# Batch 1's packed queries in the first p load, batch 4's keys and queries turned by the DMA crossbar, and a new order of the work

## The chip, the cores and the metric

The kernel runs on one core of one Trainium2 chip. The metric is the device time of that core in microseconds (us), as the median of the runs shown. The core's engines are TensorE (PE), VectorE (DVE), ScalarE (ACT), GpSimd (POOL) and SyncE (SP); each works through its own queue of instructions in order, and 16 DMA engines move the data. Here POOL issues nearly all loads and SP nearly all stores and the transposing DMAs.

## The reference

```python
def sm_attn(qq, kk, vv):
    s = scale * np.matmul(qq, kk.transpose(0, 1, 3, 2))      # scale = 1/8
    a = np.exp(s - np.max(s, axis=-1, keepdims=True))
    a = a / (np.sum(a, axis=-1, keepdims=True) + 1e-09)
    return np.matmul(a, vv)

p_packed = sm_attn(p, k, v)              # p [8, 8, 32, 64]; q, k, v [8, 8, 576, 64]
o = sm_attn(q, p_packed, p_packed)       # [8, 8, 576, 64]
x = o.transpose(0, 2, 1, 3).reshape(4608, 512)
h = x @ w_in                             # [512, 2048]
out = (np.maximum(h, 0.0) ** 2) @ w_out  # [2048, 512], out is [4608, 512]
```

Inputs and output are float32. There are 8 batches of 8 heads. For each head, 32 learned "packed queries" p attend to 576 keys, and the 576 queries then attend to the 32 packed results. Two dense layers with a squared ReLU between them follow, over all 4608 tokens.

## The kernel before

**Stages of a batch.** The work is cut into pieces with short names, and the prediction uses these names. For a batch b and a half qd of its heads:

- Loads by POOL: Lk (keys), Lv (values), Lq (queries), LWI and LWO (w_in and w_out); functions `dma_kq` (655), `dma_v` (674), `x_v` (679), `dma_w_in` (691), `dma_w_out` (695). LP is a load of p (`p_load`, 635), P its cast (642), PT its turn on VectorE (646).
- Tk and Tq turn keys and queries so that the head dimension lies on the partitions. For batches 0 to 4 VectorE does it (`tr_k`, L705, and `tr_q`, L702). For the batches in XBAR (5, 6, 7) a transposing DMA does it, which SP issues (`xbar`, L711); p then goes the same way, in two such DMAs, PX.0 and PX.1 (`xbar_p`, L715), and the values come in six loads and two zero fills rather than two loads.
- S1 is p times keys (L733; L749 in a crossbar batch), MX the row maximum (L752), EX the exponential (L760), E the turn of the result (L766), EC its copy, PV the product with the values (L780), RC and XN the normalisation (L784, L787), XM the turn of p_packed (L796; in a crossbar batch also L799), XC its copy.
- M multiplies p_packed with w_in ahead of time (L810): the second attention's output and the first layer become one product. Four pieces, each copied out by MC (L611 on ACT, L613 on DVE).
- S2 is queries times p_packed (L827; L837 in a crossbar batch); SI, SM, SU, SE, SS, SN and SO are its softmax and its turn (L848 to L875).
- F (batches 0 and 1, L912) or F1 (L884) is the first layer; R and Q or SQ the ReLU and the square (L894, L896, L902, L904, L920 to L932). F2 (L938) is the second layer for a tile of 128 tokens, 16 matmuls; FC copies its result out (L611, L613), and ST stores it (`store`, L950, two DMAs a tile). For tokens of batches 2 to 7 the second layer goes by groups of 256 tokens with sums of operands (GS, L990; WS, L983; products GP, L1005, 8 matmuls a piece; GC, L1025 and L611, adds them up).

**What sets the order.** Nothing is a loop over batches at run time: a list scheduler (`Plan`, lines 31 to 217) orders all pieces while the program is built. Every piece has one or more engines with a cost in us, the pieces that it follows, the PSUM halves that it takes, and a due level; TABLE (from line 228) holds an offset to the level of each piece. TURN is a cost that the planner adds where TensorE goes from one form of matmul to another. `run` (199) then emits the pieces in planned order, engine by engine, and puts filler matmuls (L617) into planned idle time of TensorE before the second layer begins.

The planned order is only an order on each engine. At run time an instruction waits for the data that it reads, for the buffer that it writes, and for the slot of its DMA queue; nothing waits for a planned time.

**Loads.** ORDER gives their sequence; x and y are the halves of batch 0's queries, a the parts of w_in, b those of w_out:

```python
ORDER = ("k0 v0 x0 a0 y0 a1 a2 a3 k1 b0 b1 v1 b2 q1 b3 b4 b5 b6 b7 "
         "k2 v2 q2 k3 v3 q3 k4 v4 q4 k5 v5 q5 k6 v6 q6 k7 v7 q7")
```

An entry "p4" in ORDER would give the load behind it, in the plan, the batch's Tk, Tq and, for the first crossbar batch, PX as pieces to follow.

**The packed queries.** p comes in three loads: batch 0 (64 KB, issued by ACT at the very start), batch 1 (64 KB, issued by SP behind a gate, a one-column write of VectorE) and batches 2 to 7 (issued by SP behind a second gate). They land in space that the gT sums and the w_out sums use later (gS, wS).

Of the kernel before, what the change touches and what calls it, by code (L numbers as in the profile page):

```python
# [11 lines left out]
F32 = mybir.dt.float32  # L12
BF16 = mybir.dt.bfloat16

P = 128
D = 64
# [10 lines left out]
TURN = 0.098  # L27
# [14 lines left out]
class Plan:  # L42
# [170 lines left out]
    def fills(self, a, b):  # L213
        if b - a < 0.7:
# [6 lines left out]
         "k2 v2 q2 k3 v3 q3 k4 v4 q4 k5 v5 q5 k6 v6 q6 k7 v7 q7")  # L221

KHW = 2
GROUPS = (2, 3, 4, 5, 6, 7)
XBAR = (5, 6, 7)
XTURN = (5, 6, 7)

TABLE = {'o': {'Lk.0.0i': 118.526678, 'Lk.0.1i': -2.097617, 'Lk.0.0': 127.028834, 'LP.0': -27.492568, 'Lk.0.1':
# [295 lines left out]
def kernel_impl(tc, q, k, v, p, w_in, w_out, out):  # L524
# [23 lines left out]
    with ExitStack() as ctx:  # L548
# [517 lines left out]
        for x in ORDER.split():  # L1066
# [29 lines left out]
            elif x[0] == "a":  # L1096
                for i in range(2):
                    for qd in QDS:
                        load(f"LWI.{n}.{i}.{qd}", 0.7, lambda n=n, i=i, qd=qd: dma_w_in(n, i, qd), 0.6)
# [297 lines left out]
```

## Time and profile before

| quantity | value |
|---|---|
| runs | 238.29, 238.25, 237.69 us; median 238.25 |
| profiled execution | 239.7 us |
| its span, first to last instruction | 237.9 us |
| mean granted TensorE clock in it | 0.997 |
| share of the chain that ended last, TensorE | 77% |
| data moved by DMA | 34.06 MB |

The table's span is what the profile's own times count from; the 1.8 us between it and the execution's time lie before the first and behind the last instruction. Where a view lists groups, it gives the line of the kernel, the engine, the operation, the output and inputs, the count, and then the busy time and the mean duration in ns. Where it lists stretches, it gives for each engine the busy time and, in brackets, the number of instructions.

### The profile page before, as it was taken

What the parts mean: (1) busy time and instruction counts of PE and PEld (TensorE: products, weight loads), DVE (VectorE), ACT (ScalarE), POOL (GpSimd) and SP (SyncE); (2) the same over time, 40 slices, a digit from 0 to 9 for tenths busy, and PEclk for the clock granted to TensorE, in tenths of its full rate; (3) what the DMA queues carried; (4) which work ended last, traced back from release to release, by engine and by line L of the source; (5) the groups of instructions that cost most, each with busy time, mean ns of one, the idle gap of its engine ahead of it and who ended that gap; (6) DMA issues with size and microseconds to landing.
All of it is one profiled execution on the core that took longest, in us unless ns stands there. A gap on an engine that the chain in (4) does not pass through costs nothing.

```text
span 237.9 us, 6410 instructions
## 1 busy us (share of the span) xinstructions
PE 223.7 (94%) x2635; PEld 159.6 (67%) x2635; DVE 201.4 (85%) x337; ACT 149.6 (63%) x242; POOL 59.9 (25%) x107
## 2 busy tenths in 40 slices
PE   7778798999999999999999999999999999999991
PEld 5555564435644547677678878788676888888781
DVE  3678797899799999999978999999999997868240
ACT  3314795179858999959797363449979987400100
POOL 9778546333343658600000000000000000000000
PEclk9999999999999999999999999999999999999998
DMA  7999999999999999998147697860314000615316
GB/s 226 175 179 176 190 204 204 204 195 248 239 204 229 213 224 212 199 203 129 38 96 140 141 163 165 189 130 4 88 44 92 3 0 0 146 33 110 69 42 178
DMA packets 46732, 34.06 MB, mean 143 GB/s; under 512 B 25392, under 2 KB 38448, under 8 KB 46704
## 3 DMA queue, kind: packets, MB, share of 16 engines
q0 software_dynamic: 19456, 18.03, 47.5%
q1 hardware_dynamic: 26576, 15.05, 29.7%
q10 hardware_dynamic: 672, 0.59, 1.0%
q8 instruction: 20, 0.33, 0.6%
q14 instruction: 8, 0.07, 0.1%
HBM read 37.22 MB, written 9.44 MB: 196 GB/s over the span
## 4 chain that ended last, share of the span: by engine, by line
PE 77%; DMA 10%; ACT 4%; POOL 2%; DVE 2%; issue 1%; SPq 1%; DVEq 0%; POOLq 0%
PE pb L1005 29%; PE ps L884 20%; PE pb L938 12%; DMA w_in_b<-in_moe_w_in_dram 6%; PE ps L810 3%; PE ps L912 3%; PE ps L938 3%; DMA v_b<-in_v_dram 3%; DMA out_dram<-o_sb 2%; ACT r_b L920 2%; PE pb L956 1%; PE ps L827 1%; PE ps L780 1%; PE ps L733 1%; POOL w_in_b L693 1%
## 5 line engine op out<-in xcount | busy, mean ns | idle before, releaser
L894 ACT ACTIVATE r_b<-ps 128x576 bf16<-128x576 f32 x86 | 50.1, 663 | 12.5 <-PE ps L884 12.2
L884 PE MATMUL ps<-a,M 128*128 128x288 bf16 x384 | 53.0, 286 | 0.0
L884 PEld LDWEIGHTS <-M 128*128 128x128 bf16 x384 | 37.3, 98 | 11.5 <-DVE a L875 0.3
L1005 PEld LDWEIGHTS <-gT 128*128 128x128 bf16 x384 | 37.1, 98 | 7.3 <-issue 2.5
L938 PE MATMUL pb<-w_out_b,gT 128*128 128x512 bf16 x144 | 39.1, 380 | 0.0
L611 ACT CAST M<-ps 128x1024 bf16<-128x1024 f32 (+1 forms) x29 | 26.5, 950 | 10.2 <-PE ps L810 8.8
L950 POOL DMA_DIRECT2D out_dram<-o_sb x2 | 1.1, 570 | 122.7 <-DVE o_sb L1025 121.5
L1005 PEld LDWEIGHTS <-gS 128*128 128x128 bf16 x288 | 27.6, 98 | 4.6 <-issue 0.9
L611 ACT COPY o_sb<-pb 128x512 f32<-128x512 f32 (+1 forms) x21 | 12.0, 571 | 29.4 <-PE pb L1005 18.8
L904 DVE TENSOR_TENSOR gT<-r_b 128x1152 bf16<-128x1152 bf16 x36 | 26.4, 747 | 3.6 <-ACT r_b L894 3.5
L1025 DVE TENSOR_TENSOR o_sb<-o_sb,pb 128x512 f32<-128x512 f32 x30 | 20.3, 677 | 9.3 <-PE pb L1005 8.5
L938 PEld LDWEIGHTS <-gT 128*128 128x128 bf16 x176 | 16.0, 98 | 15.9 <-issue 3.0
L1005 PE MATMUL pb<-wS,gT 128*128 128x256 bf16 x192 | 23.9, 273 | 0.5 <-DVE o_sb L1025 0.5
L1005 PE MATMUL pb<-wS,gS 128*128 128x256 bf16 x192 | 24.0, 273 | 0.0
L1005 PE MATMUL pb<-w_out_b,gT 128*128 128x256 bf16 x192 | 23.3, 273 | 0.0
L912 PE MATMUL ps<-a,M 128*128 128x256 bf16 (+3 forms) x160 | 19.5, 262 | 2.1 <-DVE M L613 0.6
L912 PEld LDWEIGHTS <-M 128*128 128x128 bf16 x160 | 13.9, 97 | 8.1 <-issue 2.5
L920 ACT ACTIVATE r_b<-ps 128x512 bf16<-128x512 f32 (+2 forms) x25 | 15.5, 662 | 3.8 <-PE ps L912 3.0
L861 ACT ACTIVATE e<-s 128x1152 bf16<-128x1152 f32 (+4 forms) x11 | 10.0, 909 | 10.3 <-DVE s L858 10.2
L760 ACT ACTIVATE e<-ps,n 128x576 bf16<-128x576 f32 x16 | 11.8, 744 | 7.4 <-DVE n L752 5.9
L617 PE MATMUL pb<-o_sb 128*128 128x256 bf16 x91 | 13.2, 299 | 1.1 <-DVE o_sb L620 1.1
L902 ACT ACTIVATE gT<-r_b 128x1152 bf16<-128x1152 bf16 x12 | 14.0, 1177 | 0.1
(88 smaller groups left out, 337.0 us busy)
## 6 DMA issues: line engine op xcount, KB each, us to landing
out_dram<-o_sb SPq DMA_DIRECT2D x65, 128.0 KB, 3.1
kq_b<-in_k_dram POOLq DMA_DIRECT2D x14, 288.0 KB, 9.8
kq_b<-in_q_dram POOLq DMA_DIRECT2D x10, 288.0 KB, 6.5
w_in_b<-in_moe_w_in_dram POOLq DMA_DIRECT2D x16, 128.0 KB, 6.1
w_out_b<-in_moe_w_out_dram POOLq DMA_DIRECT2D x8, 256.0 KB, 9.2
v_b<-in_v_dram POOLq DMA_DIRECT2D x5, 320.0 KB, 10.3
v_b<-in_v_dram POOLq DMA_DIRECT2D x12, 128.0 KB, 8.2
v_b<-in_v_dram POOLq DMA_DIRECT2D x5, 256.0 KB, 10.3
```

The source lines that it names most:

```text
L611: nc.scalar.copy(dst, src)
L617: nc.tensor.matmul(half(7)[:, :2 * P], lhsT=zero[:, :P], rhs=zero, start=True, stop=True)
L760: nc.scalar.activation(e_out(qd) if b in XBAR else e1[:, qd, :S], ps1[b, qd], ACT.Exp, bias=n1[b % 2][:, qd:qd + 1], accum_out=d1[b % 2][: ...
L884: nc.tensor.matmul(t[:, c], lhsT=M[b % 2][:, qd, fb * FB:(fb + 1) * FB], rhs=a2[b % 2][:, qd, c * HALF:(c + 1) * HALF], start=(qd == 0), s ...
L894: nc.scalar.activation(dst, src, ACT.Relu)
L902: nc.scalar.activation(dst, r, ACT.Square)
L904: eng.tensor_tensor(out=dst, in0=r, in1=r, op=ALU.mult)
L912: nc.tensor.matmul(t[:, c, m * w:(m + 1) * w], lhsT=M[b % 2][:, qd, fb * FB:(fb + 1) * FB], rhs=a2[b % 2][:, qd, o:o + w], start=(qd == 0) ...
L920: nc.scalar.activation(dst, ph["h", b, x, j], ACT.Relu)
L938: nc.tensor.matmul(po[t], lhsT=gT[:, fb, n0:n0 + P], rhs=w_out_b[:, fb, :], start=(fb == 0), stop=(fb == NFB - 1))
L1005: nc.tensor.matmul(pz[g, k][:, i], lhsT=a[:, f, i * P:(i + 1) * P], rhs=w[:, f], start=(k not in ON and h == 0 and f == 0 and i == 0), sto ...
L1025: nc.vector.tensor_tensor(out=oC(g, i, j), in0=oC(g, *src), in1=pz[g, z], op=ALU.add)
```

## The change

Four things change in the code.

1. p is loaded in two parts instead of three: batches 0 and 1 at the start by ACT (128 KB), batches 2 to 7 by SP. The load of batch 1 by SP and its gate go.
2. XBAR is (4, 5, 6, 7) instead of (5, 6, 7). Batch 4's keys and queries are turned by SP's transposing DMAs instead of VectorE; its values come in six loads and two zero fills; its S1, XM and S2 take the crossbar form; PX.0 and PX.1 hold one batch more.
3. "p4" stands behind q4 in ORDER.
4. Costs in the planner and TURN are new, and every offset in TABLE is new. The order on all engines differs with it.

```diff
-TURN = 0.098
+TURN = 0.111
...
-         "k2 v2 q2 k3 v3 q3 k4 v4 q4 k5 v5 q5 k6 v6 q6 k7 v7 q7")
+         "k2 v2 q2 k3 v3 q3 k4 v4 q4 p4 k5 v5 q5 k6 v6 q6 k7 v7 q7")
...
-XBAR = (5, 6, 7)
+XBAR = (4, 5, 6, 7)
...
-            p_f += [gS[:, i].rearrange("p a n -> p (a n)")[:, :2 * NQD * D].bitcast(F32) for i in range(2)]
+            p_f.append(gS[:, 0].rearrange("p a n -> p (a n)")[:, :2 * 2 * NQD * D].bitcast(F32))
...
-        for i, n, gate in ((1, 1, "MX.0.1"), (2, 6, "XQ.1")):
+        for i, n, gate in ((1, 6, "XQ.1"),):
...
-        for i, (b0, b1) in enumerate(((0, 1), (1, 2), (2, B))):
+        for i, (b0, b1) in enumerate(((0, 2), (2, B))):
...
-                add(f"S1.{b}", [("PE", 0.3, lambda u0, u1, b=b: x1_mm(b, [u0, u1]))], [f"Tk.{b}.0", f"Tk.{b}.1", "PX.0", "PX.1"],
+                add(f"S1.{b}", [("PE", 0.26, lambda u0, u1, b=b: x1_mm(b, [u0, u1]))], [f"Tk.{b}.0", f"Tk.{b}.1", "PX.0", "PX.1"],
...
-        p_load(0, 0, 1, nc.scalar)
+        p_load(0, 0, 2, nc.scalar)
```

The other costs that change are those of LP.0 (0.25 to 0.5), three of the w_in loads (0.45 more each), S1 (0.56 to 0.51), PV (0.5 to 0.3), XM (0.17 to 0.33 and 0.07 to 0.06), M (0.235 to 0.216) and S2.

In instructions as built: TensorE has 32 matmuls fewer at L733 and at L827, 32 more at L749, 16 more at L837, two more at L799, and 13 more fillers (104 instead of 91). VectorE has two turns fewer at L705 and two fewer at L702. POOL has six more loads of values in place of two, and two more zero fills. SP has four more transposing DMAs of keys and queries.

In the built order, SP's queue around batch 4 reads: the load of p for batches 2 to 7; the stores of tiles 0, 1, 2, 3, 4, 5, 7; Tk.4.0, PX.0, PX.1, Tk.4.1, Tq.4.0, Tq.4.1; the stores of tiles 8, 6, 11, 12, 9, 10; Tk.5.0, Tk.5.1. Before, PX.0 and PX.1 stood behind Tk.5.0 and Tk.5.1. On TensorE, S1.4 now stands behind the first seven F2 matmuls of tile 6 and then F1.2, one F2 matmul more among them, and one GP piece; before, it stood ahead of F1.2 (at 78.57 us).

More of the change, by code (lines that the diff above doesn't have):

```diff
@@ L220 @@
 ORDER = ("k0 v0 x0 a0 y0 a1 a2 a3 k1 b0 b1 v1 b2 q1 b3 b4 b5 b6 b7 "
-         "k2 v2 q2 k3 v3 q3 k4 v4 q4 k5 v5 q5 k6 v6 q6 k7 v7 q7")
+         "k2 v2 q2 k3 v3 q3 k4 v4 q4 p4 k5 v5 q5 k6 v6 q6 k7 v7 q7")
 KHW = 2
 GROUPS = (2, 3, 4, 5, 6, 7)
-XBAR = (5, 6, 7)
+XBAR = (4, 5, 6, 7)
 XTURN = (5, 6, 7)
-TABLE = {'o': {'Lk.0.0i': 118.526678, 'Lk.0.1i': -2.097617, 'Lk.0.0': 127.028834, 'LP.0': -27.492568, 'Lk.0.1':
[293 rows of a table removed]
+TABLE = {'o': {'Lk.0.0i': 5.480127, 'Lk.0.1i': 1.259675, 'Lk.0.0': -2.731651, 'LP.0': 11.399977, 'Lk.0.1': -10.074651,
[293 rows of a table added]
 def kernel_impl(tc, q, k, v, p, w_in, w_out, out):
@@ L562, in kernel_impl @@
         v_b = many("v_b", NV, [P, H, (GM + 1) * D], BF16)
-        p_f = [] if GROUPS else [consts.tile([P, n * D], F32, name=f"p_f{i}") for i, n in enumerate((2, 2, 12))]
+        p_f = [] if GROUPS else [consts.tile([P, n * D], F32, name=f"p_f{i}") for i, n in enumerate((4, 12))]
         if GROUPS:
@@ L1058, in kernel_impl @@
             add("Lk.0.0", [("DMA", 2.0, None)], ["Lk.0.0i"], line="dma", lag=0.55, level=-300)
-        add("LP.0", [("DMA", 0.25, None)], line="dma", lag=0.8, level=-299)
+        add("LP.0", [("DMA", 0.5, None)], line="dma", lag=0.8, level=-299)
         if KHW > 1:
@@ L1098, in kernel_impl @@
                     for qd in QDS:
-                        load(f"LWI.{n}.{i}.{qd}", 0.7, lambda n=n, i=i, qd=qd: dma_w_in(n, i, qd), 0.6)
+                        load(f"LWI.{n}.{i}.{qd}", 0.7 + 0.45 * ((n, i, qd) in ((1, 0, 0), (3, 0, 0), (3, 1, 1))), lambda n=n, i=i, qd=qd: dma_w_in(n, i, qd), 0.6)
             else:
                 load(f"LWO.{n}", 1.42, lambda n=n: dma_w_out(n), 0.73)
-        for i, n, gate in ((1, 1, "MX.0.1"), (2, 6, "XQ.1")):
+        for i, n, gate in ((1, 6, "XQ.1"),):
             add(f"G.{i}", [("DVE", 0.06, lambda i=i: p_gate(i))], [gate], level=-99)
-            add(f"LP.{i}i", [("SP", 0.5, lambda i=i, b0=(0, 1, 2, B)[i], b1=(0, 1, 2, B)[i + 1]: p_load(i, b0, b1, nc.sync))], [f"G.{i}"], lag=1.0, level=-99)
+            add(f"LP.{i}i", [("SP", 0.5, lambda i=i, b0=(0, 2, B)[i], b1=(0, 2, B)[i + 1]: p_load(i, b0, b1, nc.sync))], [f"G.{i}"], lag=1.0, level=-99)
             for x in range(n):
@@ L1143, in kernel_impl @@
             for i in range(2):
-                add(f"PX.{i}", [("SP", 1.5, lambda i=i: xbar_p(i))], ["P.2"] + (["P.1"] if X0 == 2 else []) + quiet.get(X0, issued[-1:]), lag=XLAG, level=-5)
+                add(f"PX.{i}", [("SP", 1.5, lambda i=i: xbar_p(i))], ["P.1"] + quiet.get(X0, issued[-1:]), lag=XLAG, level=-5)
         for b in range(B):
@@ L1154, in kernel_impl @@
                     ([f"Lk.{b}.{qd}"] if b or qd >= KHW else [f"KC.{qd}.0", f"KC.{qd}.1"]) + ([f"S1.{b - 1}" if b > 1 else f"S1.0.{qd}"] if b else []), line="Tk", level=L)
-            pt = f"PT.{min(b, 2)}"
+            pt = f"PT.{int(b > 1)}"
             if b in XBAR:
-                add(f"S1.{b}", [("PE", 0.3, lambda u0, u1, b=b: x1_mm(b, [u0, u1]))], [f"Tk.{b}.0", f"Tk.{b}.1", "PX.0", "PX.1"],
+                add(f"S1.{b}", [("PE", 0.26, lambda u0, u1, b=b: x1_mm(b, [u0, u1]))], [f"Tk.{b}.0", f"Tk.{b}.1", "PX.0", "PX.1"],
                     line="S1", take=[PAIRS, PAIRS], mode=3, level=L + 1)
@@ L1163, in kernel_impl @@
             else:
-                add(f"S1.{b}", [("PE", 0.56, lambda u0, u1, b=b: s1_mm(b, [u0, u1]))], [f"Tk.{b}.0", f"Tk.{b}.1", pt],
+                add(f"S1.{b}", [("PE", 0.51, lambda u0, u1, b=b: s1_mm(b, [u0, u1]))], [f"Tk.{b}.0", f"Tk.{b}.1", pt],
                     line="S1", take=[PAIRS, PAIRS], mode=1, level=L + 1)
@@ L1178, in kernel_impl @@
                     free=[(f"E.{b}.{qd}", 0)], level=L + 1)
-            add(f"PV.{b}", [("PE", 0.5, lambda u, b=b: pv_mm(b, u))], [*([f"E.{b}"] if b in XTURN else [f"EC.{b}.0", f"EC.{b}.1"]), *([f"Lv.{b}.{i}" for i in range(6)] + [f"VZ.{b}"] if b in XBAR else [f"Lv.{b}.0", f"Lv.{b}.1"])] + (["I2"] if b else []),
+            add(f"PV.{b}", [("PE", 0.3, lambda u, b=b: pv_mm(b, u))], [*([f"E.{b}"] if b in XTURN else [f"EC.{b}.0", f"EC.{b}.1"]), *([f"Lv.{b}.{i}" for i in range(6)] + [f"VZ.{b}"] if b in XBAR else [f"Lv.{b}.0", f"Lv.{b}.1"])] + (["I2"] if b else []),
                 line="PV", take=[ONES[:3] if b < 2 else ONES], mode=2, level=L + 1)
@@ L1185, in kernel_impl @@
             gone2 = ([f"M.{b - 2}.{NWC - 1}"] + ([f"S2.{b - 2}"] if b - 2 in XBAR else [])) if b > 1 else []
-            add(f"XM.{b}", [("PE", 0.17 if b in XBAR else 0.07, lambda b=b: ppT_mm(b))], [f"XN.{b}"], level=L + 1)
+            add(f"XM.{b}", [("PE", 0.33 if b in XBAR else 0.06, lambda b=b: ppT_mm(b))], [f"XN.{b}"], level=L + 1)
             add(f"XC.{b}", either(ppT_out, *((0.31, 0.26) if b in XBAR else (0.22, 0.16)), b), [f"XM.{b}"] + gone2, free=[(f"PV.{b}", 0)], level=L + 1)
             for c in range(NWC):
-                add(f"M.{b}.{c}", [("PE", 0.235, lambda u, b=b, c=c: m_mm(b, c, u))], [f"XC.{b}"] + [f"LWI.{c}.{i}.{qd}" for i in range(2) for qd in QDS]
+                add(f"M.{b}.{c}", [("PE", 0.216, lambda u, b=b, c=c: m_mm(b, c, u))], [f"XC.{b}"] + [f"LWI.{c}.{i}.{qd}" for i in range(2) for qd in QDS]
                     + (lasts(b - 2) if b > 1 else []), line="M", take=[PAIRS], mode=3, level=L + 3)
@@ L1215, in kernel_impl @@
                     continue
-                add(f"S2.{b}.{x}", [("PE", 0.06 + 2 * tok / 2400 * 1.05, lambda u, b=b, x=x: s2_mm(b, x, u))], [f"XQ.{b}"] + tq, line="S2", take=[PAIRS], mode=1, level=l2)
+                add(f"S2.{b}.{x}", [("PE", 0.00088 * tok, lambda u, b=b, x=x: s2_mm(b, x, u))], [f"XQ.{b}"] + tq, line="S2", take=[PAIRS], mode=1, level=l2)
                 add(f"SI.{b}.{x}", [("DVE", 0.1 + w / 970, lambda b=b, x=x: s2_in(b, x))], [f"S2.{b}.{x}"] + over("SE", b, *span(b, x)), free=[(f"S2.{b}.{x}", 0)], level=l2)
             if b in XBAR:
-                add(f"S2.{b}", [("PE", 0.3, lambda u0, u1, b=b: x2_mm(b, [u0, u1]))], [f"XC.{b}"] + tq, line="S2", take=[PAIRS, PAIRS], mode=3, level=L + 2)
+                add(f"S2.{b}", [("PE", 0.245, lambda u0, u1, b=b: x2_mm(b, [u0, u1]))], [f"XC.{b}"] + tq, line="S2", take=[PAIRS, PAIRS], mode=3, level=L + 2)
                 for qd in QDS:
@@ L1267, in kernel_impl @@
                 add(f"WS.{i}.{h}", [("DVE", 0.6, lambda i=i, h=h: w_sum(i, h))],
-                    lw + ([f"WS.{(0, 0, 0, 1)[i]}.{h}"] if i in (1, 3) else []) + ([f"P.{2}"] if i == 3 else []), level=45.0, key=f"WS.{i}")
+                    lw + ([f"WS.{(0, 0, 0, 1)[i]}.{h}"] if i in (1, 3) else []) + (["P.1"] if i == 3 else []), level=45.0, key=f"WS.{i}")
         def store_any(t, part, o=slice(None)):
```

586 rows, old and new, of the table TABLE are left out of this document.

## The prediction

> **What bounds the kernel now.** I read the page's busy times first, then the engines by stage, then TensorE's fill matmuls alone, then the chain that ended last.
>
> ```profile
> span 237.9 us, 6410 instructions
> PE 223.7 (94%) x2635; PEld 159.6 (67%) x2635; DVE 201.4 (85%) x337; ACT 149.6 (63%) x242; POOL 59.9 (25%) x107
> ...
> PE 77%; DMA 10%; ACT 4%; POOL 2%; DVE 2%; issue 1%; SPq 1%; DVEq 0%; POOLq 0%
> ```
>
> TensorE holds 77% of the chain. An average hides stages, so here is each stage; the columns are the stretch, its length, then busy time (and count) of PE, PEld, DVE, ACT and POOL, the granted clock, the DMA share and GB/s:
>
> ```profile
> 0.00:27.00 27.00, 20.17 (x278) 13.60 (x278) 18.77 (x51) 10.73 (x19) 21.22 (x40) 1.00 1.08 188
> 27.00:43.00 16.00, 14.70 (x210) 9.70 (x209) 12.25 (x25) 11.19 (x20) 8.25 (x13) 1.00 1.24 204
> 43.00:67.00 24.00, 23.64 (x180) 12.21 (x172) 22.37 (x43) 16.61 (x26) 8.22 (x14) 1.00 1.19 222
> 67.00:100.00 33.00, 32.74 (x537) 18.28 (x537) 32.15 (x52) 29.81 (x51) 20.46 (x37) 1.00 1.23 214
> 100.00:214.00 114.00, 114.00 (x1294) 89.60 (x1293) 106.74 (x155) 79.38 (x123) 0.64 (x2) 1.00 0.52 96
> 214.00:237.90 23.90, 18.50 (x168) 16.16 (x166) 9.12 (x14) 1.92 (x4) 1.14 (x2) 0.98 0.40 99
> ```
>
> The same view with the keep-the-clock fills (L617) alone has 13.16 of the first 20.17 us; no other stage has fills:
>
> ```profile
> 0.00:27.00 27.00, 13.16 (x91) 9.14 (x91) 1.00 1.08 188
> 27.00:43.00 16.00, 0.00 (x0) 0.00 (x0) 1.00 1.24 204
> ```
>
> So there are three regimes. Up to 27 us TensorE does 20.17 - 13.16 = 7.0 us of real work and waits for loads. From 27 to 214 us it is TensorE's time: idle there is 1.30 (27 to 43), 0.36 (43 to 67) and 0.26 (67 to 100), 1.92 us in all. The last stage has 5.4 us of idle, at the end of the chain:
>
> ```profile
> 20.24 6.64 DMA w_in_b<-in_moe_w_in_dram
> 26.92 0.41 PE ps L810 x3
> ...
> 33.72 0.73 PE ps L733 x30
> ...
> 42.64 0.63 PE ps L827 x28
> ...
> 204.39 10.49 PE pb L1005 x96
> ...
> 217.48 4.02 DMA out_dram<-o_sb
> ```
>
> The first real regime ends when the last w_in load lands (20.24 + 6.64 = 26.88). A change can move the end only by the landing at 26.88, by those 1.92 us, by TensorE's amount of work, by a new stall, or by the tail.
>
> **The change, part by part.**
>
> *Start.* The p loads move the same bytes: 128 KB at once instead of 64 and 64, and no SP load behind a gate. The loads ahead of the last w_in load keep their order. I leave the landing at 26.88, and give it 0.3 us either way.
>
> *Order between 27 and 67 us.* The new order puts batch 0's first-layer products (F) between the M products and brings other ready work in front of S1.1 (L733 at 33.72) and S2.1 (L827 at 42.64), where TensorE idled. At most 1.30 + 0.36 = 1.66 us can go, at least nothing. I take half, -0.8: part of the idle follows chains (softmax of batch 1, through ACT and DVE) that a new order can't shorten.
>
> *Batch 4 on the crossbar, TensorE.* These rows give what a batch costs the old and the new way (columns: start, busy, instructions; the cost is from one start to the next):
>
> ```profile
> 74.33 0.70 PE L827 MATMUL ps<-qT,pq 32*32 32x256 bf16 x32
> 74.96 0.41 PE L810 MATMUL ps<-w_in_b,ppT 64*32 64x512 bf16 x8
> ...
> 78.57 0.70 PE L733 MATMUL ps<-kT,pT 32*32 32x512 bf16 x32
> 79.20 0.41 PE L810 MATMUL ps<-w_in_b,ppT 64*32 64x512 bf16 x8
> ```
>
> and, from the chain, how S1 and S2 look in a crossbar batch:
>
> ```profile
> 125.13 0.38 PE ps L749 x27
> 138.18 0.37 PE ps L837 x16
> ```
>
> S1 goes from 0.63 to 0.38 and S2 from 0.63 to 0.37; XM (L796 and L799) needs two more matmuls at 0.22 to 0.24 each by their groups below, at most +0.5. Sum: -0.25 - 0.26 + 0.3 = -0.2, between -0.5 and 0. Counting every TensorE piece of the two built orders by such costs, with 0.09 for each change of matmul form, the totals differ by +0.1, since the new order changes form more often. I take +0.1.
>
> ```profile
> L796 PE MATMUL ps<-ident,pp 128*128 128x128 bf16 x6 | 1.3, 221 | 0.4 <-DVE pp L787 0.4
> L799 PE MATMUL ps<-ident,pp 128*64 128x128 bf16 x6 | 0.7, 243 | 0.0
> L705 DVE STREAM_TRANSPOSE kT<-kq_b 128x576 f32<-128x576 f32 x10 | 7.4, 759 | 0.4 <-DMA kq_b<-in_k_dram 0.4
> L702 DVE STREAM_TRANSPOSE qT<-kq_b 128x576 f32<-128x576 f32 (+2 forms) x12 | 7.8, 660 | 0.0
> ```
>
> *VectorE* loses four transposes, 2 x 0.759 + 2 x 0.660 = 2.8 us, of 32.15 busy out of 33.00. That would pay only where TensorE waits for VectorE, and TensorE's idle there is 0.26: I count nothing for it. Should VectorE's relief be eaten by other pieces, nothing is lost either.
>
> *Batch 4's transposes on SP.* This is the term that decides. In the new SP queue stand, in this order, the two stores of token tile 7, Tk.4.0, PX.0, PX.1, Tk.4.1, Tq.4.0, Tq.4.1. S1.4 on TensorE needs the first four. The store of tile 7 waits for the copy FC.7, and that for the last F2.7 matmul. Between that matmul and S1.4 TensorE has, in the new order, 24 matmuls of F2, 8 pieces of 4 F1 matmuls, one GP piece of 8, PV.3, XM.3, four M pieces and S2.3. By the rows
>
> ```profile
> 80.10 1.89 PE L938 MATMUL pb<-w_out_b,gT 128*128 128x512 bf16 x8
> 81.82 0.22 PE L796 MATMUL pb<-ident,pp 128*128 128x128 bf16 x1
> ...
> 90.57 0.49 PE L780 MATMUL pb<-v_b,e 128*32 128x64 bf16 x40
> 91.02 1.14 PE L884 MATMUL ps<-a,M 128*128 128x288 bf16 x8
> 92.00 0.22 PE L796 MATMUL pb<-ident,pp 128*128 128x128 bf16 x1
> ```
>
> F2 is (81.82 - 80.10) / 8 = 0.215, F1 (92.00 - 91.02) / 8 = 0.122, PV 0.45; GP 10.49 / 96 = 0.109; M 0.3; S2 0.63. Sum: 24 x 0.215 + 32 x 0.122 + 8 x 0.109 + 0.45 + 0.06 + 1.2 + 0.63 = 12.3, and about 8 further changes of form, 0.7: **13.0 us of cover**.
>
> What must fit under it: the copy and two store issues (0.57 each by L950's row below; about 2.4 with the steps between), then three issues on SP and the issue-to-landing time of the fourth. The trace has both conditions, view of L711 with loads still in flight (99 to 115 us) and with none (124 to 160 us); columns min/median/max ns of the issue, then landing in us:
>
> ```profile
> L711 SPq DMA_TRANSPOSE kT<-kq_b x2: 1773/2440/3106, 100.7 to 102.7; - x2
> ...
> DMA to landing us min/median/max: 5.7/6.5/7.5
> ```
>
> ```profile
> L711 SPq DMA_TRANSPOSE kT<-kq_b x4: 1288/1305/1326, 125.6 to 137.3; - x4
> ...
> DMA to landing us min/median/max: 3.2/3.3/5.0
> ```
>
> ```profile
> L950 SPq DMA_DIRECT2D out_dram<-o_sb x67: 533/596/2067, 51.4 to 233.6; - x67
> ```
>
> Quiet: 2.4 + 3 x 1.3 + 3.3 = 9.6, 3.4 to spare. Beside loads: 2.4 + 3 x 1.77 + 5.7 = 13.4 (0.4 late) at best, 2.4 + 3 x 2.44 + 6.5 = 16.2 (3.2 late) at the median, 2.4 + 3 x 3.11 + 7.5 = 19.2 (6.2 late) at worst. Which holds depends on the pause. The planner puts the next load, k5.0, behind Tk.4, Tq.4 and PX, but a plan is no wait. In the built kernel's instructions k5.0's load waits only for a DMA queue's slot and for its buffer; the first load that waits for a batch 4 transpose stands 19 loads later (q6.1). The trace of before shows such a plan broken: q7.0's load was planned ahead of Tk.5, and was still in flight when Tk.5 was issued:
>
> ```profile
> 99.53 0.56 POOL L659 DMA_DIRECT2D kq_b<-in_q_dram  x1 [0.16 <-issue]
> ...
> 100.71 5.05 SPq L711 DMA_TRANSPOSE kT<-kq_b  x2
> ```
>
> So I expect Tk.4 beside loads at about 79 to 92 us, where the DMA share is 1.23. TensorE runs in order, so a late S1.4 adds one for one. I take 1.8 us, the middle of the loaded best and median: PX is among the four and is smaller. Ends: 0 and 6.2.
>
> The Trainium skill speaks against a need for the pause: "DMA: Bandwidth & Descriptors", Rules for kernel authors, says that a transpose next to ordinary DMAs needs nothing. It says so of correctness in the first place; the landings, 5.7 to 7.5 beside loads against 3.2 to 5.0, differ from it as to time. By that rule, read for time, the stall would be nought.
>
> *Loads.* If they don't pause, they end where they did, and Tk.5 has the same neighbours. Nothing counted.
>
> **Sum.** -0.8 + 0.1 + 1.8 = +1.1. The profiled execution took 239.7 (span 237.9 and 1.8 around it), 1.45 above the median of 238.25; it would go to 240.8, the median to **239.3**. About 0.3%, 0.7 us, is what a measurement of this kernel can tell from no change.
>
> **Rivals.**
>
> *A, a wash.* S1.4 is late by 0.4 to 1.5, as by the loaded best, and the start gives 0.8: 237.9 to 238.9. For it: 0.4 is a traced pair's best. Against it: it needs all three issues at the best.
>
> *B, the transposes stay hidden (the other side).* The place is Tk.4.1's landing against the 13.0 us of cover; it decides at an issue of about 1.65 and a landing of 5.7, or anything quicker. The quiet rows have 3.4 us to spare. Then -0.8 + 0.1 = -0.7 gives 237.5; with all of the 1.66 won 236.7, with none 238.35. For it: POOL, which issues the loads, is busy for 20.46 of the 33.00 us, so the loads come with gaps. Against it: the DMA share of 1.23. The Trainium skill, "Advanced Engine Details and Errata", X-Bar Transpose (TRN2), says that transposes on this chip go as fast as regular DMAs; by that this rival would hold, and the quiet landing of 3.3 against 3.1 for a store (the median of the page's row below) agrees with that, though not beside loads.
>
> ```profile
> out_dram<-o_sb SPq DMA_DIRECT2D x65, 128.0 KB, 3.1
> ```
>
> *C, my forecast*, 239.0 to 241.5.
>
> *D, the pause is real after all*, so that the change does what it says: the transposes are quiet (9.6, hidden), and the loads of batches 5 to 7 come some 10 us later. They would end near 116 to 120 instead of 106, Tk.5 would land some 5 us later than that, and S1.5 is at 125.13: time as B, or up to a microsecond worse. It would take a wait that the built order doesn't show, so it counts little and goes with B.
>
> **How the numbers follow.** C 0.42 (239.3), A 0.16 (238.4), B with D 0.42 (237.5; of it 0.31 below 237.5, that is faster by over 0.3%, and 0.11 within). Faster 0.31, same 0.27, slower 0.42. The likeliest case's own range is 239.0 to 241.5. The whole range goes from B with nearly all of the start's idle won, 236.8, to the loaded median with nothing won, 238.25 + 3.2 = 241.5; below it lies about 0.06, above it (the worst loaded rows) about 0.12.
>
> **What would show it.** Right: an idle of 1 to 3 us on TensorE ahead of batch 4's L749, ended by kT or pX; L711 issues of 1.8 us or more near 80 to 90 us, with POOL's loads running beside them; TensorE's idle between 27 and 67 us down by about 0.8; everything behind S1.4 shifted by one amount; the same tail. Wrong: L711 near 1.3 us with no idle at L749 (then B); POOL silent for some 10 us behind q4's loads (then D); a last w_in landing more than 0.5 us away from 26.88; or a new TensorE wait between 100 and 214 us, where I count none.

## The result and the profile after

The changed kernel takes **262.19 us** (261.12 to 264.63, 4 runs), the kernel before 238.27 in the same runs: a ratio of 1.102, 95% interval 1.0939 to 1.1101. The forecast was 239.3 with a range up to 241.5. The direction held, and for the reason given, a stall at S1.4; its size was missed by more than twenty microseconds.

The head of the page of the changed kernel:

```profile
span 260.1 us, 6409 instructions
PE 227.2 (87%) x2634; PEld 161.7 (62%) x2634; DVE 199.2 (77%) x329; ACT 146.6 (56%) x242; POOL 62.5 (24%) x112
...
PEclk9999999999999975579999999999999999999998
```

TensorE's busy time is 227.2, 3.5 more than before (1.5 of it fillers, 14.7 instead of 13.2), while the span grew by 22.2: more work on TensorE doesn't explain it. The clock's row has a dip in slices 15 to 18, that is from 91 to 117 us: TensorE stood still. The stretches say how long (columns as in the prediction: busy PE, PEld, DVE, ACT, POOL, clock, DMA share, GB/s):

```profile
27.00:43.00 16.00, 14.95 (x219) 9.04 (x217) 13.99 (x28) 10.75 (x20) 8.05 (x14) 1.00 1.24 204
43.00:67.00 24.00, 24.00 (x187) 13.03 (x186) 23.33 (x45) 16.96 (x29) 7.73 (x14) 1.00 1.19 227
67.00:100.00 33.00, 22.68 (x352) 11.73 (x350) 21.64 (x34) 20.41 (x32) 15.28 (x28) 0.91 1.35 161
100.00:130.00 30.00, 19.29 (x228) 13.32 (x227) 16.66 (x26) 16.14 (x29) 7.42 (x14) 0.76 1.25 130
```

From 67 to 130 us TensorE is idle for 10.3 + 10.7 us. In that time the DMA engines are as busy as ever (share 1.35 and 1.25) but move 161 and 130 GB/s where the kernel before moved 214 between 67 and 100. TensorE's list of waits names one instruction:

```profile
PE ps L749 <- DMA kT<-kq_b: 11.7, 1, 11.7
PE ps L749 <- DMA pX<-p_b: 8.8, 1, 8.8
```

L749 is S1 of a crossbar batch, here S1.4, the place that the prediction named. It waited 8.8 us for PX and 11.7 more for Tk.4.1: 20.5 us. The view of L711 (turns of keys and queries; issue ns min/median/max, then landing us) between 70 and 120 us, and SP's timeline (start, time in the queue):

```profile
L711 SPq DMA_TRANSPOSE kT<-kq_b x2: 2093/5779/9465, 78.4 to 89.8; - x2
L711 SPq DMA_TRANSPOSE qT<-kq_b x2: 4766/5422/6078, 99.5 to 104.4; - x2
...
DMA to landing us min/median/max: 15.6/16.4/20.3
```

```profile
78.39 2.09 SPq L711 DMA_TRANSPOSE kT<-kq_b  x1
80.53 9.07 SPq L715 DMA_TRANSPOSE pX<-p_b  x2
89.77 9.46 SPq L711 DMA_TRANSPOSE kT<-kq_b  x1
```

Tk.4.0 was issued at 78.39, as the prediction's chain had it. Then each crossbar DMA held SP's queue for 2.1 to 9.5 us and landed 15.6 to 20.3 us after its issue. POOL's timeline shows its loads beside them:

```profile
79.16 0.56 POOL L659 DMA_DIRECT2D kq_b<-in_q_dram  x1
80.84 0.55 POOL L659 DMA_DIRECT2D kq_b<-in_q_dram  x1 [1.11 <-DMA v_b<-in_v_dram]
81.37 1.06 POOL L659 DMA_DIRECT2D kq_b<-in_k_dram  x2
...
98.53 0.58 POOL L685 DMA_DIRECT2D v_b<-in_v_dram  x1 [7.54 <-DMA kq_b<-in_q_dram]
```

The pause isn't there. POOL goes on issuing loads up to 101.7 us, and slows down only because its own loads land late (7.54 us of waiting for one); the first load that a crossbar DMA holds up goes out at 110.6, when Tk.4.1 has landed.

**Where the 22 us came from.** Take the place of a matmul in the run, less the time that the TensorE pieces ahead of it cost by the prediction's rows; the difference between the kernels is what waiting cost. By F1.2's first matmul (87.33 before, 84.12 after, with 0.7 us less work ahead of it) this profile is 2.5 us ahead; 0.8 of it belongs to the profile of the kernel before, a run of 239.7, since another run of that order (238.46, the load of p alone, below) has this matmul at 86.53. S1.4 costs 21.1 (the 20.5 of waiting, and 31 of its matmuls at a low clock). From there to F1.2's sixteenth piece, at 119.6 us, it loses 2.5 more; 0.6 of this is a wait for batch 4's EC that the new order has without the collision too (shown further below), and over the rest the clock and the other engines' queues recover. Later waits cost 0.75 more than before. -2.5 + 21.1 + 2.5 + 0.75 = 21.9; the last matmul ends at 254.98 instead of 233.02.

### The profile page after: what moved, and what is told of

Same layout as the page of the kernel before. It is cut to its first block, busy times and chain, and to the rows that moved or that the text cites. A ratio compares the mean times of both kernels' runs of the same rounds, so it can differ in the third digit from the quotient of the medians.

```text
span 260.1 us, 6409 instructions
## 1 busy us (share of the span) xinstructions
PE 227.2 (87%) x2634; PEld 161.7 (62%) x2634; DVE 199.2 (77%) x329; ACT 146.6 (56%) x242; POOL 62.5 (24%) x112
## 4 chain that ended last, share of the span: by engine, by line
PE 69%; DMA 13%; DVE 8%; SPq 5%; ACT 2%; issue 1%; DVEq 0%; ACTq 0%
PE pb L1005 23%; PE ps L884 17%; PE pb L938 11%; DMA kT<-kq_b 8%; PE ps L912 5%; SPq L715 3%; DMA out_dram<-o_sb 3%; PE ps L938 3%; PE ps L810 3%; DMA gT<-in_k_dram 2%; PE pb L956 1%; SPq L950 1%; DVE o_sb L1025 1%; PE ps L733 1%; PE ps L780 1%
## 5 line engine op out<-in xcount | busy, mean ns | idle before, releaser
L894 ACT ACTIVATE r_b<-ps 128x576 bf16<-128x576 f32 x92 | 52.8, 669 | 30.4 <-PE ps L884 30.1
L884 PEld LDWEIGHTS <-M 128*128 128x128 bf16 x384 | 37.4, 99 | 11.9 <-issue 1.1
L611 ACT CAST M<-ps 128x1024 bf16<-128x1024 f32 (+1 forms) x31 | 27.8, 934 | 14.2 <-PE ps L810 11.7
L904 DVE TENSOR_TENSOR gT<-r_b 128x1152 bf16<-128x1152 bf16 x42 | 31.0, 754 | 5.5 <-ACT r_b L894 5.3
L752 DVE TENSOR_REDUCE n<-ps 128x1 f32<-128x576 f32 x16 | 11.4, 752 | 22.1 <-PE ps L749 21.1
L611 ACT COPY o_sb<-pb 128x512 f32<-128x512 f32 (+1 forms) x20 | 11.4, 572 | 29.6 <-PE pb L1005 17.9
L1005 PE MATMUL pb<-w_out_b,gT 128*128 128x256 bf16 x192 | 24.5, 279 | 0.0
L749 PE MATMUL ps<-kT,pX 64*32 64x256 bf16 (+1 forms) x128 | 2.4, 244 | 20.5 <-DMA kT<-kq_b 11.7
L912 PE MATMUL ps<-a,M 128*128 128x256 bf16 (+3 forms) x160 | 18.6, 262 | 1.9 <-DVE a L875 1.3
L760 ACT ACTIVATE e<-ps,n 128x576 bf16<-128x576 f32 x16 | 11.7, 734 | 9.6 <-DVE n L752 9.6
L920 ACT ACTIVATE r_b<-ps 128x512 bf16<-128x512 f32 (+2 forms) x24 | 14.6, 645 | 3.3 <-PE ps L912 3.1
L617 PE MATMUL pb<-o_sb 128*128 128x256 bf16 x104 | 14.7, 300 | 1.1 <-DVE o_sb L620 1.1
```

The source lines that it names most:

```text
L611: nc.scalar.copy(dst, src)
L617: nc.tensor.matmul(half(7)[:, :2 * P], lhsT=zero[:, :P], rhs=zero, start=True, stop=True)
L752: nc.vector.tensor_reduce(n1[b % 2][:, qd:qd + 1], ps1[b, qd], axis=AX.XY if b in XBAR else AX.X, op=ALU.max, negate=True)
L760: nc.scalar.activation(e_out(qd) if b in XBAR else e1[:, qd, :S], ps1[b, qd], ACT.Exp, bias=n1[b % 2][:, qd:qd + 1], accum_out=d1[b % 2][: ...
L884: nc.tensor.matmul(t[:, c], lhsT=M[b % 2][:, qd, fb * FB:(fb + 1) * FB], rhs=a2[b % 2][:, qd, c * HALF:(c + 1) * HALF], start=(qd == 0), s ...
L894: nc.scalar.activation(dst, src, ACT.Relu)
```

## The experiments

**Theory 1**: transposing DMAs and POOL's loads slow each other while they run together, and nothing but the plan kept them apart. **Theory 2**: the six in a row are slow at this place by themselves, or (2b) the new order is bad by itself.

### The pause made real

```diff
+    # ahead of batch 5's first key load, in POOL's queue, for one column each of kT[:, 0..1], pX[0..1], qT[:, 0..1]:
+    nc.gpsimd.tensor_copy(gs_b[:, i:i + 1], column)
```

> The changed kernel, with the pause made real: ahead of batch 5's first key load POOL reads one column of kT, pX and qT as batch 4's crossbar DMAs leave them, so that POOL's loads wait for them. Theory 1 (loads and crossbar DMAs that run together slow each other; the pause was only in the plan): POOL falls silent from about 82 us; batch 4's DMAs move once the loads of v4 and q4 have landed, near 88; the wait ahead of S1.4 falls from 20.5 to 3 to 6 us, the time to 239 to 243. Theory 2 (the crossbar DMAs are slow in this place by themselves, six in a row behind stores in one queue; the loads have no part): the wait stays at 18 to 21 us, the time at 258 or more.

**239.13 us** (238.10 to 240.84), ratio 1.0026 (0.9994 to 1.0057): the same as the kernel before. S1.4 doesn't wait at all. POOL's timeline and the view of L711 between 60 and 125 us (the third kT is batch 5's):

```profile
72.02 0.55 POOL L659 DMA_DIRECT2D kq_b<-in_q_dram  x1 [0.89 <-DVE ppT L613]
81.99 0.19 POOL L1054 COPY gs_b<-kT 128x1 bf16<-128x1 bf16 x1 [9.42 <-DMA kT<-kq_b]
...
90.74 1.06 POOL L659 DMA_DIRECT2D kq_b<-in_k_dram  x2 [0.27 <-issue]
```

```profile
L711 SPq DMA_TRANSPOSE kT<-kq_b x3: 1328/1431/2542, 78.4 to 123.9; - x3
L711 SPq DMA_TRANSPOSE qT<-kq_b x2: 1331/1340/1348, 85.4 to 86.9; - x2
...
DMA to landing us min/median/max: 3.3/3.4/4.7
```

The loads stop for 18 us, and the same DMAs, issued at the same 78.4 us in the same queue, land in 3.3 to 4.7 us. Theory 2 is out: 23 of the 24 us go with the overlap. The expectation was wrong in one thing, a remaining wait of 3 to 6 us: I had taken POOL's loads at 79 to 82 us for batch 4's, but they are batch 5's; batch 4's had landed by 78 (the last one issued at 72.02, landed 6.0 us later). The late loads cost nothing: the last one goes out at 127.8 us instead of 108.8, and S1.5 doesn't wait.

### How much overlap it takes

The same gate, put two loads later (behind batch 5's keys), and ten loads later (behind all of batch 5).

```diff
-GATES = {"Lk.5.0": ...}
+GATES = {"Lv.5.0": ...}      # two loads later
+GATES = {"Lk.6.0": ...}      # ten loads later
```

> The changed kernel with the real pause two loads later: POOL reads kT, pX and qT ahead of batch 5's first value load, so that only the two key loads of batch 5 (issued near 72 to 73 us) can be beside batch 4's crossbar DMAs (from 78.4 us). Theory 1 with a dose (the collision lasts as long as loads are in flight): these two have landed by about 80; the crossbar DMAs then land as in the run with the full pause (3.3 to 4.7 us), no wait at S1.4, 238 to 240. If any load at all beside them spoils the whole row of six: a wait of 5 us or more, 245 or more.

> The same with the real pause ahead of batch 6's first key load: ten loads more than in the full pause (keys, values and queries of batch 5, about 1.8 MB as read) are in flight or issued when Tk.4.0 is issued. Theory 1 with a dose: the two sorts slow each other until these loads have landed, near 92 to 98 us; S1.4, due near 89, waits 4 to 12 us; 243 to 252, between the full pause (239.1) and none (262.2). If the slowness came with the later loads only (those issued beside or behind the crossbar DMAs): no wait, 238 to 240.

Two loads: **238.84 us** (ratio 1.0022, 0.9991 to 1.0053), no wait. The two were issued at 72.1 and 72.8 us, and the last landed at 79.7, 0.8 us after Tk.4.0 was issued: almost no overlap. Ten loads: **248.71 us** (247.93 to 250.95; ratio 1.0439, 1.0389 to 1.0489). The view of L711 between 60 and 125 us with ten loads, and TensorE's waits at S1.4:

```profile
L711 SPq DMA_TRANSPOSE kT<-kq_b x2: 3628/4815/6002, 79.1 to 88.2; - x2
L711 SPq DMA_TRANSPOSE qT<-kq_b x2: 1300/1318/1335, 94.5 to 95.9; - x2
...
DMA to landing us min/median/max: 3.2/5.7/15.0
```

```profile
PE ps L749 <- DMA pX<-p_b: 4.8, 1, 4.8
PE ps L749 <- DMA kT<-kq_b: 1.2, 1, 1.2
```

In one kernel both regimes stand side by side: up to 88 us, with loads in flight, 3.6 to 6.0 us an issue and a landing of 15.0; from 94 us, when they have landed, 1.3 and 3.2. The last of the ten landed at 94.3, and Tk.4.0 at 94.1: the long landing ended when the loads did. So the time is 239, 239, 249 and 262 us with none, two, ten and all of the loads let through.

### Which DMA it is that collides

```diff
-nc.sync.dma_start_transpose(t[:, qd]..., kq_of[nm, b, qd][:])
+nc.sync.dma_start(t[:, qd]..., kq_of[nm, b, qd][:])      # batch 4 and PX only
```

> The changed kernel, without a real pause, with batch 4's six crossbar DMAs replaced by plain DMAs of the same bytes between the same tiles (SBUF to SBUF, not turned, so that S1 and S2 of batch 4 and S1 of batches 5 to 7 work on other data). Theory 1a (what collides with the loads is the transposing DMA, with its 256-byte packets): the plain ones land in 5 to 8 us beside the same loads, as the stores do, S1.4 waits 0 to 3 us, 237 to 242. Theory 1b (any DMA of SP beside POOL's loads at this place gets slow): landings of 12 us or more, a wait of 10 us or more, 250 or more.

**240.63 us** (239.37 to 241.75; ratio 1.0075, 1.005 to 1.0101). S1.4 waits 1.4 us instead of 20.5: it is the transposing DMA that collides with the loads, and not just any DMA of SP's. The plain copies land in 6.2 to 11.9 us, later than the 5 to 8 expected, but each holds SP's queue for 0.5 us (PX 0.9) rather than 2.1 to 9.5. The DMA view of one window, 78.4 to 98.1 us, in the kernel before, the changed kernel and this one (packets and bytes of all, then of POOL's queue q0 and of SP's q1):

```profile
DMA packets 4795, 4.24 MB, mean 215 GB/s; under 512 B 1432, under 2 KB 3437, under 8 KB 4791
...
q0 software_dynamic: 4311, 3.39, 112.2%
q1 hardware_dynamic: 480, 0.79, 11.9%
```

```profile
DMA packets 4670, 2.63 MB, mean 133 GB/s; under 512 B 2673, under 2 KB 4072, under 8 KB 4669
...
q0 software_dynamic: 2558, 1.86, 87.1%
q1 hardware_dynamic: 2111, 0.75, 52.2%
```

```profile
DMA packets 5240, 4.83 MB, mean 245 GB/s; under 512 B 1466, under 2 KB 3770, under 8 KB 5238
...
q0 software_dynamic: 4054, 2.79, 93.5%
q1 hardware_dynamic: 1184, 2.00, 30.6%
```

With the transposing DMAs, the loads move 1.86 MB instead of 3.39 and SP's queue only 0.75; with plain ones 2.79 and 2.00. The number of packets is nearly the same in all three (4670 to 5240): what a transposing DMA's small packets take from the loads, they don't give back in bytes. Alone, with the real pause, they are not slow (78.4 to 90.6 us there: 6222 packets in 12.2 us). The Trainium skill, "DMA: Bandwidth & Descriptors", Queues, rings and completion order, says that each DMA engine takes turns between its queues packet by packet. The near equal counts of the changed kernel, 2558 of the loads' queue and 2111 of SP's, would fit that; whether the profile's packet is the page's isn't shown. Why a packet costs more in the mix than alone, no run here shows, nor whether loads that another engine issues would collide too: the loads here are POOL's.

### The order without batch 4's crossbar DMAs

```diff
-("SP", XUS, lambda b=b, qd=qd: xbar(kT, "k", b, qd))
+("SP", XUS, None if b == 4 else lambda b=b, qd=qd: xbar(kT, "k", b, qd))      # Tq.4 and PX likewise
```

> The changed kernel without batch 4's six crossbar DMAs (Tk.4, Tq.4, PX left out; kT and qT keep what batch 3 left, pX is set to zero; so S1 to S2 of batch 4, and S1 of batches 5 to 7, work on other data). Theory 1: no wait at S1.4, the loads run as in the kernel before and end near 104 to 107 us; 235 to 237, which is what the new order gives without the collision. Theory 2b (the order is bad): 240 or more.

**239.06 us** (238.16 to 240.47; ratio 1.0004, 0.9973 to 1.0034). No collision and no loss, so theory 2b is out too; but no gain of 2 us either, as I had expected from the one profile. Its profiled execution, at 240.47 the slowest of its ten, was late from the start. The two timelines of TensorE at the start, first the changed kernel, then this one (its lines are shifted by 3):

```profile
16.83 0.58 PE L827 MATMUL ps<-qT,pq 32*32 32x192 bf16 x28 [0.59 <-DVE qT L702]
17.34 1.70 PE L617 MATMUL pb<-o_sb 128*128 128x256 bf16 x14
18.97 0.90 PE L810 MATMUL ps<-w_in_b,ppT 64*32 64x512 bf16 x8
```

```profile
18.13 0.86 PE L830 MATMUL ps<-qT,pq 32*32 32x192 bf16 x28 [1.67 <-DVE qT L705]
18.93 3.03 PE L617 MATMUL pb<-o_sb 128*128 128x256 bf16 x14
21.89 0.41 PE L813 MATMUL ps<-w_in_b,ppT 64*32 64x512 bf16 x8
```

S2.0 waits for batch 0's last queries. Here they came 1.3 us later, the 14 fillers behind it ran at a low clock (3.03 us instead of 1.70; granted clock 0.54 from 18.9 to 21.9 us), and the next M began 2.9 us later. The start of the new order hangs on a landing that varies.

That isn't why the median gained nothing. F1.2's first matmul stands at 86.53 us in the profile of the old order nearest its median (238.46), and in the new order at 84.10 to 84.80 in seven of nine profiles (85.43 and 86.76, this run's, in the others). About 0.7 us of this is work that now stands behind it; 1.0 to 1.7 is a gain. It is spent behind F1.2. The two rows are the old order's, then that of the kernel with the pause made real; the waits, in the same order, are TensorE's behind these rows:

```profile
86.53 0.65 PE L884 MATMUL ps<-a,M 128*128 128x288 bf16 x4
84.10 2.61 PE L884 MATMUL ps<-a,M 128*128 128x288 bf16 x20
```

```profile
PE pb L1005 <- DVE o_sb L1025: 0.2, 1, 0.2
```

```profile
PE pb L1005 <- DVE o_sb L1025: 1.2, 2, 0.7
PE ps L884 <- ACT e L611: 0.6, 1, 0.6
```

From F1.2's first matmul to the end of the span the old order takes 150.2 us in this profile (236.7 - 86.53) and 150.6 in that of the kernel before; the new order takes 151.9 to 153.2 in the five profiles without a collision. Of what it takes longer, 0.7 is the moved work. In the pair shown the difference is 2.8, and 1.6 of it are these waits, at 96.7, 151.9 and 221.4 us (the last one varies in the old order too, 0.2 and 0.5); what is left isn't followed up.

### Two tries to make the start steadier

```diff
+self.keep(4 if p.name in ("M.0.1", "M.0.2") else self.fills(...))      # with the real pause: fewer fillers
+key=... LWI.0.1.1i ... if p.name == "I"                                  # with the pause two loads later: identity behind the fourth w_in load
```

> The kernel with the full real pause (239.1), with 4 fillers each ahead of M.0.1 and M.0.2 instead of 14 and 17. Its runs spread from 238.1 to 240.8, and in the run without batch 4's crossbar DMAs, which has the same order, M.0.1 began 2.5 us later than in the changed kernel's profile, behind a query load that landed 1.3 us later and 14 fillers that ran at a low clock. If these fillers hand on the lateness of the load: the spread shrinks and the median falls to 237.5 to 238.5. If the last w_in load sets this stage anyway: the same time within 0.3.

> The kernel with the real pause behind batch 5's key loads (238.84), with POOL's making of the identity matrix moved back behind the fourth w_in load, where the kernel before has it. Its runs spread from 237.8 to 241.9, those of the kernel before from 237.8 to 239.6. If the early identity, which holds up two w_in loads by about 0.7 us, is behind the late starts: the spread shrinks to that of before and the median falls by 0.3 to 0.8, to 238.0 to 238.5. If the spread comes from TensorE's order at the start, which waits for the second part of batch 0's queries: the same within 0.3.

Fewer fillers: 239.20 us (237.37 to 241.29; ratio 1.0018, 0.9991 to 1.0045). Identity moved: 239.14 us (238.76 to 240.90; ratio 1.0023, 1.0002 to 1.0045). Neither moves the median. The second halves the spread (2.1 us between its ends, 4.1 with the identity early), so the identity may have a part in it, but not at the median; the rest stays open. No version here beats the kernel before.

### The load of p alone

```diff
-p_load(0, 0, 1, nc.scalar)      # kernel before, its own order; batch 1's load, gate, cast and turn left out
+p_load(0, 0, 2, nc.scalar)
```

> The kernel before, in its own order, with p loaded in two parts only (batches 0 and 1 at the start). If the load of p has no part in the result: 238.25 within 0.7. If the bigger first load delays S1.0, or the early p of batch 1 lets S1.1 come sooner: 0.3 to 1.5 us either way.

**238.49 us** (238.05 to 238.85; ratio 0.9995, 0.9979 to 1.0011): no part of the result.

### Two that tell little

The changed kernel with XBAR (5, 6, 7) and without p4:

```diff
-XBAR = (4, 5, 6, 7)
+XBAR = (5, 6, 7)
```

> The changed kernel with XBAR (5, 6, 7) and no p4: batch 4's keys and queries turned by VectorE again, all costs and offsets as in the change; TensorE's order is that of the changed kernel up to S1.3, then the scheduler's own. Theory 1: nothing of the 24 us is left, and TensorE's gain of 2.5 us by F1.2 in the changed kernel stays: 235.5 to 237.5. Theory 2b (the new order is bad in itself, also without the crossbar): 240 or more.

**266.37 us** (ratio 1.1161, 1.1105 to 1.1218). The offsets belong to the plan with batch 4 on the crossbar; with one piece of it undone, the scheduler makes another, worse order. In its worst stretch VectorE is busy for 27.2 of 30 us and TensorE for 21.3:

```profile
100.00:130.00 30.00, 21.26 (x232) 14.49 (x231) 27.19 (x34) 12.02 (x15) 6.10 (x11) 0.82 0.68 111
```

It says nothing of the crossbar at S1.4, and the expectation was wrong. It does show the collision once more, at another place: batch 5's two key transposes, issued at 86.6 and 89.3 us with loads beside them, held SP's queue for 2.6 and 4.9 us and landed 11.3 to 17.0 us after their issue.

The changed kernel with TensorE kept busy through its wait:

```diff
+for _ in range(180 if b == 4 else 0):      # ahead of S1.4's matmuls, into their PSUM space
+    nc.tensor.matmul(pair(us[0])[:, 0, :2 * P], lhsT=zero[:, :P], rhs=zero, start=True, stop=True)
```

> The changed kernel with 180 filler matmuls (about 19 us at full clock) ahead of S1.4, into the PSUM space that S1.4 then overwrites, so that TensorE is busy through most of its wait. In the changed kernel TensorE lost 20.5 us waiting at S1.4 and 3.3 us more by the time that it had caught up, where the granted clock was 0.5 to 0.7. If the clock is behind these 3.3 us: they go, and the time is 259 to 260. If they come from the queues of the other engines that have to start again: no change, 262 within 1.

263.07, 263.68 and 257.04 us: too far apart for a verdict. In its profile the clock stayed at 1.00 up to 112 us, but kT landed at 113.4 instead of 110.2, TensorE waited the last 3.0 us without fillers, and the clock fell again. From F1.2's ninth piece to its sixteenth it took 8.3 us, the changed kernel 8.9, the one with the real pause 6.8. One profile, of a kernel whose three runs lie 6.6 us apart, and in which the clock fell all the same, doesn't say what part of the 2.1 us is the clock's: that stays open.

## Why the prediction was right and wrong, step by step

- **The bound and the place**: right. TensorE's path decided, and S1.4 is where it was lost.
- **"A plan is no wait"**: right, and it was the whole matter. With the pause made real, 23 of the 24 us go.
- **The load of p, TensorE's amount of work, VectorE's relief**: taken as next to nothing. The first was measured alone, at 0.9995; the other two weren't, but nothing in the runs without a collision (0.26% from the kernel before at most) speaks against them.
- **The start, -0.8**: right about the place and nearly the size, wrong about the end. TensorE's idle time between 27 and 67 us fell from 1.66 us to 1.05 here, and from 2.51 to 1.66 between the two runs compared above. But the prediction put any new wait further on at nothing. Without a collision the new order waits 1.8 us behind F1.2 in the profile shown, the old one 0.2, and so the term adds next to nothing to the total: 1.0004 (0.9973 to 1.0034) without the collision.
- **The cover of 13.0 us and Tk.4.0's issue**: right to within 0.3. F2.7's last matmul began at 76.1 us and TensorE ran dry at 89.3, 13.2 later (13.0 forecast); Tk.4.0 was issued at 78.39, 2.3 behind it (2.4).
- **The stall at S1.4, 1.8 with ends at 0 and 6.2**: this is the step that failed; it measured 20.5. Its form was right: with the measured terms, 2.3 to Tk.4.0's issue, 11.4 for the three issues (5.3 to 9.3 forecast) and 20.3 for the fourth's landing (5.7 to 7.5 forecast), it gives 34.0 against 13.2 of cover. What was wrong is the price of an issue and of a landing beside loads. In the stretch of the kernel before that they were read from, POOL issued a load at 99.53 and then nothing until 108.76. That load, the last in flight, landed at 105.8, and Tk.5.0 and Tk.5.1 at 108.2 and 109.2, 2.4 and 3.4 us later, where a quiet landing takes 3.2 to 5.0. As these times suggest, and as the run with ten loads repeats, the row held what was left of a few loads, plus little more than a quiet transfer. Where loads keep coming, nothing ends the overlap: 15.6 to 20.3 us. Of its three landings, 7.5 and 6.5 are Tk.5.0's and Tk.5.1's; the 5.7, which I took as the best case of Tk.4.1, is that of Tq.5.0, issued at 109.14 beside a single load. I used the spread of one situation as the bounds of another.
- **Rival B**, the transposes hidden: it needed an issue of about 1.65 us and a landing of 5.7, or quicker, beside the loads, and met 2.1 to 9.5 and 15.6 to 20.3.
- **Rival D**, the pause real, at 237.5 or up to a microsecond worse: its mechanism is what the gate shows, at 239.1: the pause costs nothing (S1.5 doesn't wait). Its chance was set low for the right reason, that the built order has no such wait.
- **The rule that a transpose next to ordinary DMAs needs nothing** (the Trainium skill, "DMA: Bandwidth & Descriptors", Rules for kernel authors): no help for time. The measurement is 3.3 to 4.7 us alone, 15.6 to 20.3 beside loads.

## What to carry to other kernels

A scheduler's dependency on "the load before" orders instructions; it keeps no transfer away from another. Where quiet is needed, make it a data dependence: six one-column copies in POOL's queue were worth 23 us here. And before a duration is used as a price, ask what ended it: a wait that ended because the other traffic ended says nothing of traffic that goes on. A gain early in a chain counts only when nothing behind it waits longer: look for it at the end, not where it was made.

## What the runs showed that I had not expected

- Transposing DMAs and loads together moved 133 GB/s in a window where loads and stores moved 215 and loads with plain copies 245; both sorts lost.
- A transposing DMA beside loads also holds its queue: up to 9.5 us an issue, 1.3 alone, 0.5 for a plain copy of the same bytes. Everything behind it in SP's queue waits, stores too.
- After 20 us of waiting, TensorE needed some 2 us more to be back at its pace.
